# Block 0 of a fused linear-attention and hard-swish kernel: chunks 2 and 3 read in parts, the second pair's down product by seven products

## The chip, the cores and the metric

The kernel runs on one core of a Trainium2 chip. The metric is the device time of one execution in microseconds. Engines are named as in the profile: PE (TensorE, matmuls), PEld (its weight loads), DVE (VectorE), ACT (ScalarE), POOL (GpSimd), SP (SyncE, which issues nearly all DMAs). A line number such as L824 is a line of the kernel before the change.

## The reference

Two parts are computed one after the other. The first is a recurrence over 768 tokens for 4 batches and 8 heads of 48 elements; the second is a feed-forward layer over the 3072 resulting tokens with 384 inputs and 2048 hidden columns.

```
for t in range(S):
    cur = einsum('bhd,bhe->bhde', u * k[t], v[t])
    y[t] = einsum('bhd,bhde->bhe', r[t], state + cur)
    state = w[t][..., None] * state + einsum('bhd,bhe->bhde', k[t], v[t])
x = y as (3072, 384)
h = x @ w_in                      # 384 x 2048
g = h * clip(h + 3, 0, 6) / 6
out = g @ w_out                   # 2048 x 384
```

All data are in 32-bit floats, except that the two weight matrices arrive as 64-bit floats, which the kernel turns into 32-bit floats itself.

## The kernel before

**Tiling.** The 3072 tokens are 24 chunks of 128 (`L`); `NT` is 24, the chunk's index is `i`. Two batches run side by side, so chunks 0 and 1 are both the first of their batch (`is_first`). Four chunks make a block (`BC`), so there are six blocks (`bk`). A chunk's 8 heads lie as 4 pairs (`P`) on 112 partitions: head 2p on partitions 0 to 47 and head 2p+1 on partitions 64 to 111.

**A chunk.** Its steps have short names in the planner, with the index behind: `feat` and `tok` load it; `back` and `fore` are two scans on DVE (L422, L431) that give the running products of the decays; `K` and `R` multiply them in (L442, L446; on DVE for chunks 0 to 6, on POOL after that); `own`, `dot`, `sum` and `diag` make the diagonal (L455, L465, L471, L481); `score` multiplies keys with queries (L490) and `above` copies the upper triangle into the matrix A (L497); `turn` and `turned` transpose K; `kv` makes the chunk's own outer products (L590), `kvs` takes them out of PSUM (L601, or L599), and `decay`, `mid`, `decb` and `state` update the state (L519, L527, L535). The result y is the sum of a product with the state (`read_state`, L568) and one with the values (`read_values`, L577), and `leave` copies it to `xT`, the input of the feed-forward layer.

**Where y goes.** `xT` has three column tiles of 128 rows, and the last of the four head pairs has to be spread over them. A block has two ways for this. Chunks 0 and 1 of block 0 (those below `BY_SUM`) go by parts: `first` computes the last pair alone (`read_last`), `third` copies it out on ACT (`leave_last`), and `read` (`read_rest`) adds it to the other three pairs by six matmuls with a selection matrix (L649), followed by the state and value products of the three pairs. All other chunks are read in one run and left as four copies (L677), and when both chunks of a pair are there, six small DMAs on SP (`last_pair`, L684; steps `move`) bring the last pair's rows to their places.

**The kv product.** Where a chunk is in `SOLO`, its `kv` is a step of its own; otherwise it is done at the end of the `read` of an earlier chunk, in free columns of that chunk's PSUM tile `y_ps`. Chunk 1 (`KV_APART`) has its own in two PSUM banks and two copies out (L599).

**The feed-forward layer in blocks 1 to 5.** The up product goes by 20 products instead of 24 per half (`up_product`, L824), for which DVE makes sums of the weights once (`sum_w`, L770 to L776; steps `sin0` to `sin20`) and sums of the inputs per block (`sum_x`; steps `tx`). The sums whose target is a `w` place overwrite `w_in` and wait until block 0's up products are all done. The down product is taken for two chunks at a time (a pair `p`) by seven products of half width instead of eight (`down_product`, L879), with sums of the weights (`sum_out`, L800; steps `sout1` to `sout4`, two halves each) and sums of the activations per pair (`sum_g`, L864; four kinds, two halves each), and seven reads (`down_read`; one copy L888, four scaled copies L895, two on DVE L897). `sout3` overwrites a part of `w_out` and waits for all plain down products of block 0.

**The feed-forward layer in block 0.** It goes the plain way: `up` (L710) for 16 row groups f and two pairs of chunks, `ramp` (L700) and `gate` (L721), then `down` (L729): for each of the four chunks 16 matmuls of 384 columns, and `drain` (L736) and `store`. Every 32-bit matmul shows as two instructions in the profile.

**What sets the order.** `Plan.order` is a list scheduler: each step has an engine, an assumed duration, what it follows, a key (a due time) and the buffers that it holds; among the steps that could start first on an engine it takes the one with the smallest key. Keys come from constants at the top (`START` for chunks 0 to 5, `OWN` for the diagonal, `CONV` for the weights' conversion, `UP` for block 0's up products, `SUMS` for the weights' sums, `LAG`, `AHEAD`, `LEAD`, `READ`, `GATE`, `TX` for the later blocks). `Plan.emit` writes the steps out in that order, and until block 0's first up product it puts dummy matmuls (`spin`, L1247) where the plan shows PE idle: `FILL` times the hole, divided by `SPIN` (0.25 us).

```
for _ in range(int(self.FILL * (self.start[n] - last) / self.SPIN) if n != self.until else 0):
    self.spin()
```

The tile of the selection matrix and the tile of the activations' sums share the one buffer `S_`; the gated activations of a block lie in two large tiles `g0` and `g1`, which the next block's up product fills again.

Of the kernel before, what the change touches and what calls it, by code (L numbers as in the profile page):

```python
# [18 lines left out]
L = 128  # L19
# [5 lines left out]
GBC = 3  # L25


LAG = 12.679
AHEAD = -7.562
LEAD = 5.403  # L30
BEHIND = (-1, -1, -1, 0, 6, 7)
BY_PE = 9
OWN = -16.106
SOLO = (0, 1, 2, 3, 4, 5)
EARLY = 7
APART = 1
KV_APART = (1,)
BY_SUM = 2
START = (-165.91, -200.65, -51.72, -167.86, 44.69, 31.26)
CONV = (-77.31, 6.92)  # L40
UP = (-66.42, 3.35, 14.73, 4.86)
SUMS = (157.11, 42.24, -10.72)
READ = 4.918
GATE = 10.716
TX = -15.408
LEAST = 2.0 ** -60


# [186 lines left out]
def fast_path(tc, feat, tok, wflat, ub, ug, moe_w_in, moe_w_out, out, flag, n_chunks):  # L235
# [21 lines left out]
    with ExitStack() as ctx:  # L257
# [283 lines left out]
        def new_y(i, alone=False):  # L541
            started = set()
            if i == APART and not alone:
                st[i].update(started=started, y_ps=[bank()[:, :P * HL].rearrange("q (p t) -> q p t", p=P) for _ in range(2)])
                return
            y_ps = pp.tile([128, 2, 512], F32, name="y_ps")
            if not alone:
                y_ = y_ps[:, :, :P * HL].rearrange("q a (p t) -> q a p t", p=P)
                st[i].update(started=started, y_ps=[y_[:, a] for a in range(2)], y_all=y_)
            j = i if alone else i + 1 if i < BC else i + 2  # L550
            if j < NT and (alone or j not in SOLO):
# [28 lines left out]
        def write(i):  # L580
            d = st[i]
            for p in range(P):
                for a in range(1 if is_last(i) else 2):
                    for g in range(2):

                        half = slice(a * HL, (a + 1) * HL)
                        cols = slice(g * GP, GP if g == 0 else PR)
                        fresh = (a, g * GP) not in d["kv_started"]
                        d["kv_started"].add((a, g * GP))
                        nc.tensor.matmul(d["kv_ps"][a][cols, p, :] if i in KV_APART else d["kv_ps"][cols, a, p, :], lhsT=d["kn"][half, p, cols],  # L590
                                         rhs=d["v"][half, 2 * p + g, :], start=fresh, stop=True, skip_group_check=True)

        def written(i):
            d = st[i]
            m = 1 if is_last(i) else 2
            d["kvs"] = wk.tile([PR, 2, P, D], F32, name="kvs", bufs=1)
            if i in KV_APART:
                for a in range(m):
                    nc.scalar.copy(out=d["kvs"][:, a], in_=d["kv_ps"][a])  # L599
                return  # L600
            nc.scalar.copy(out=d["kvs"][:, :m].rearrange("q a p e -> q a (p e)"),  # L601
                           in_=d["kv_ps"][:, :m].rearrange("q a p e -> q a (p e)"))

        def write_alone(i):
            if i in KV_APART:
                st[i].update(kv_started=set(), kv_ps=[bank()[:PR, :P * D].rearrange("q (p e) -> q p e", p=P) for _ in range(2)])
            else:
                new_y(i, True)
            write(i)

        def begin(i):
# [57 lines left out]

        def leave(i):  # L670
            bk, c = divmod(i, BC)
# [179 lines left out]
        def sum_g(bk, p, k, x):  # L851

            b = blocks[bk]
            m = HF // 2
            if k == 1 and x == 0:
                b["S", p] = wk.tile([128, HF, L], F32, name="S_", bufs=1)
            S = b["S", p][:, x * m:(x + 1) * m, :]

            def part(h, c):
                return b["g", p][:, h * HF + x * m:h * HF + (x + 1) * m, c * L:(c + 1) * L]  # L860
            (a11, a21), (a12, a22) = ([part(h, c) for c in range(2)] for h in range(2))
            o, x0, x1, op = {1: (S, a21, a22, ALU.add), 2: (S, S, a11, ALU.subtract), 3: (a21, a11, a21, ALU.subtract),
                             4: (S, a12, S, ALU.subtract)}[k]
            nc.vector.tensor_tensor(out=o, in0=x0, in1=x1, op=op)  # L864
# [93 lines left out]
        def do(fn, *args):  # L958
            return lambda: fn(*args)
# [25 lines left out]
        for i in range(NT):  # L985
# [40 lines left out]
            plan.add(f"turned{i}", "ACT", 0.42, do(turned_k, i), [turned_by(i)] + [f"turned{i - 1}"] * (i > 0), due - 2 if i > BC + 1 else due + 0.5,  # L1026
                     [("kn", [written_by(i)])])
            if i in SOLO:
                plan.add(f"kv{i}", "PE", 0.5, do(write_alone, i), [f"turned{i}", f"tok{i}"], t - 0.2,
                         [("bank", [f"kvs{i}"])] * 2 if i in KV_APART else [("y", [f"kvs{i}"])])  # L1030
            plan.add(f"kvs{i}", "ACT", 0.37 if i not in KV_APART else 0.5, do(written, i), [written_by(i)], t - 6 if i >= len(START) else t - 0.5,
                     [("kvs", [f"decb{i}"] if last else [f"state{i}"])])
            S_ = [("S", [f"read{i}" if i < BC else f"begin{i}"] + [f"state{i}"] * (not last))]
            if not first:
# [12 lines left out]
            y = [("y", [f"leave{i}"] + [f"kvs{with_}"] * (with_ < NT and with_ not in SOLO))]  # L1047
            if i == APART:
                y = [("bank", [f"leave{i}"])] * 2
            if i < BY_SUM:  # L1050
                plan.add(f"first{i}", "PE", 0.65 if first else 0.75, do(read_last, i), [f"above{i}", f"decb{i}"], t + 0.01, y)
                plan.add(f"third{i}", "ACT", 0.54 if i != APART else 0.9, do(leave_last, i), [f"first{i}"], t + 0.01,
                         ([("x", all_up), ("S_", [f"read{j}" for j in range(BY_SUM)])] if i == 0 else []))
# [21 lines left out]
            if c % 2 and i >= BY_SUM:  # L1075
                for g in range(2):
                    plan.add(f"move{bk}.{c // 2}.{g}", "SP", 1.8, do(last_pair, bk, c - 1, c + 1, g, nc.sync),
                             [f"leave{i - 1}", f"leave{i}"], when(i) - 50, kb=1, dmas=3)

        plan.add("u", "SP", 0.45, load_u, ["fetch3"], -60.0, kb=320)  # L1080
        plan.add("later", "SP", 0.45, load_rest, ["feat0"], key=-999.0, kb=630)
# [10 lines left out]
                plan.add(f"full{j}", "DVE", 0.87, do(high_low, j), [f"join{j}", f"whole{j}"], t, port=True)  # L1092
        ready = "full" if f64 else "fetch"

        classic = range(BC)
        all_down = [f"down0.{c}.{q}" for c in classic for q in range(HF)]
        part_of = {c: c0 for c0, c1 in parts for c in range(c0, c1)}
        for x, (c0, c1) in enumerate(parts):
            m = c1 - c0
            for f in range(NFC):  # L1100
                k = UP[2 * x] + f * UP[2 * x + 1]
                n_ = f"0.{f}.{c0}"
                plan.add(f"up{n_}", "PE", 0.645 * m, do(up, f, c0, c1), [f"{ready}{f // 2}"] + [f"leave{j}" for j in range(c0, c1)] + [f"move0.1.{g}" for g in range(2)] * (c0 >= BY_SUM),
                         k, [("bank", [f"gate{n_}"])])
                plan.add(f"ramp{n_}", "ACT", 0.1 + 0.135 * m, do(ramp, f, c0, c1), [f"up{n_}"], k - 3, [("clip", [f"gate{n_}"])])
                plan.add(f"gate{n_}", "DVE", 0.07 + 0.134 * m, do(gate, f, c0, c1),
# [37 lines left out]
        for bk in range(NB):  # L1144
# [7 lines left out]
            for d in range(2 * (bk > 0)):  # L1152
# [39 lines left out]
                for x in range(8):  # L1192
# [394 lines left out]
```

## Time and profile before

| | |
|---|---|
| median of three runs | 559.42 us (557.51 to 560.03) |
| the profiled execution | 560.03 us; its span 558.3 us |
| busy: PE / DVE / ACT / POOL | 543.8 / 435.8 / 265.2 / 108.2 us |
| mean granted PE clock | 0.982 |
| first up product of block 1 | at 145.8 us |

The span is the time from the first to the last instruction; the rest, 1.7 us, lies around it. PE counts as busy while it works at half clock and while a pipelined matmul waits inside it, and the dummy matmuls count too. Nearly the whole of what the change touches lies before 148 us, in block 0.

### The profile page before, as it was taken

What the parts mean: (1) busy time and instruction counts of PE and PEld (TensorE: products, weight loads), DVE (VectorE), ACT (ScalarE), POOL (GpSimd) and SP (SyncE); (2) the same over time, 40 slices, a digit from 0 to 9 for tenths busy, and PEclk for the clock granted to TensorE, in tenths of its full rate; (3) what the DMA queues carried; (4) which work ended last, traced back from release to release, by engine and by line L of the source; (5) the groups of instructions that cost most, each with busy time, mean ns of one, the idle gap of its engine ahead of it and who ended that gap; (6) DMA issues with size and microseconds to landing.
All of it is one profiled execution on the core that took longest, in us unless ns stands there. A gap on an engine that the chain in (4) does not pass through costs nothing.

```text
span 558.3 us, 13179 instructions
## 1 busy us (share of the span) xinstructions
PE 543.8 (97%) x5460; PEld 477.0 (85%) x5460; DVE 435.8 (78%) x717; ACT 265.2 (48%) x653; POOL 108.2 (19%) x111
## 2 busy tenths in 40 slices
PE   8999999999999999999999999999899999999996
PEld 8888766777688899888999888999788899988995
DVE  7969999999989967889968899967967817087440
ACT  3868782456377415456516456525447520255100
POOL 2000000046165015202053026232401000000000
PEclk9869999999999999999999999999989999999998
DMA  8948941633243282466335694036300000100001
GB/s 275 297 131 212 296 167 43 177 107 112 81 120 100 95 227 75 134 225 166 92 83 185 221 266 123 20 116 206 91 1 7 4 8 15 43 1 1 1 15 48
DMA packets 23269, 64.06 MB, mean 115 GB/s; under 512 B 3216, under 2 KB 10544, under 8 KB 23200
## 3 DMA queue, kind: packets, MB, share of 16 engines
q1 hardware_dynamic: 23072, 63.12, 37.8%
q8 instruction: 45, 0.74, 0.6%
q14 instruction: 24, 0.20, 0.1%
q10 hardware_dynamic: 128, 0.00, 0.0%
HBM read 57.31 MB, written 4.72 MB: 111 GB/s over the span
## 4 chain that ended last, share of the span: by engine, by line
PE 81%; DVE 11%; DMA 3%; ACT 2%; issue 1%; POOL 0%; DVEq 0%; POOLq 0%; ACTq 0%
PE bank L824 26%; PE bank L879 26%; PE bankS L824 5%; PE bankS L879 5%; PE bank L710 4%; PE bank L729 3%; DMA bits<-in_moe_w_out_dram 3%; PE bank L490 2%; PE y_ps L568 2%; PE y_ps L590 2%; PE bankS L1247 2%; PE ps L506 2%; PE y_ps L577 2%; PE ps L465 1%; DVE E L422 1%
## 5 line engine op out<-in xcount | busy, mean ns | idle before, releaser
L845 ACT ACTIVATE clip<-g,three 128x512 f32<-128x512 f32 x80 | 56.6, 720 | 44.5 <-DVE g L841 30.9
L841 DVE TENSOR_TENSOR g<-bank,g 128x512 f32<-128x512 f32 x80 | 53.7, 683 | 14.4 <-PE bank L824 10.7
L849 DVE SCALAR_TENSOR_TENSOR g<-clip,g 128x512 f32<-128x512 f32 x80 | 55.9, 714 | 7.3 <-ACT clip L845 7.3
L879 PE MATMUL bank<-w_out,g 128*128 128x192 f32 x320 | 56.7, 327 | 0.0
L879 PEld LDWEIGHTS bank<-w_out,g 128*128 128x128 f32 x320 | 52.8, 190 | 0.6
L442 POOL TENSOR_TENSOR K<-feat_in,E 112x512 f32<-112x512 f32 x17 | 22.0, 1293 | 150.0 <-DVE rk L455 100.4
L481 ACT ACTIVATE A<-eyes,dg 128x64 f32<-128x64 f32 x192 | 48.9, 335 | 1.5 <-PE y_ps L577 0.9
L710 PE MATMUL bank<-xT,w_in 128*128 128x256 f32 x192 | 47.4, 397 | 0.8 <-DMA xT<-xT 0.8
L677 ACT COPY xT<-y_ps 48x256 f32<-48x256 f32 x88 | 32.2, 366 | 31.8 <-PE y_ps L577 30.8
L729 PE MATMUL bank<-w_out,g 128*128 128x384 f32 x128 | 45.0, 493 | 0.3 <-DVE w_out L409 0.3
L710 PEld LDWEIGHTS bank<-xT,w_in 128*128 128x128 f32 x192 | 36.9, 198 | 8.9 <-DVE g L721 1.6
L895 ACT ACTIVATE o<-bank 128x192 f32<-128x192 f32 x30 | 9.9, 330 | 69.9 <-PE bank L879 69.9
L824 PE MATMUL bank<-xT,w_in 128*128 128x256 f32 x160 | 41.1, 380 | 0.0
L446 POOL TENSOR_TENSOR W<-feat_in,W 112x512 f32<-112x512 f32 x17 | 24.1, 1419 | 86.3 <-DVE W L431 86.3
L839 ACT COPY g<-bank 128x512 f32<-128x512 f32 x50 | 29.0, 580 | 18.7 <-PE bank L824 18.6
L729 PEld LDWEIGHTS bank<-w_out,g 128*128 128x128 f32 x128 | 23.4, 190 | 13.5 <-DVE w_out L409 0.4
L824 PEld LDWEIGHTS bank<-xT,w_in 128*128 128x128 f32 x160 | 30.2, 190 | 4.1
L422 DVE TENSOR_TENSOR_SCAN E<-feat_in,back 112x520 f32<-112x520 f32 x24 | 30.9, 1288 | 2.9 <-POOL K L442 1.6
L824 PE MATMUL bank<-xT,bits 128*128 128x256 f32 x120 | 31.0, 381 | 0.0
L431 DVE TENSOR_TENSOR_SCAN W<-feat_in,start 112x520 f32<-112x520 f32 x24 | 30.4, 1268 | 0.8 <-PE y_ps L568 0.7
L879 PE MATMUL bankS<-w_out,g 128*128 128x192 f32 x160 | 28.0, 328 | 0.4 <-ACT bankS L888 0.4
L879 PE MATMUL bank<-more,g 128*128 128x192 f32 x160 | 28.1, 328 | 0.0
(279 smaller groups left out, 1140.7 us busy)
## 6 DMA issues: line engine op xcount, KB each, us to landing
feat_in<-in_feat_dram SPq DMA_DIRECT2D x23, 675.9 KB, 6.7
bits<-in_moe_w_in_dram SPq DMA_DIRECT2D x8, 768.0 KB, 7.5
bits<-in_moe_w_out_dram SPq DMA_DIRECT2D x8, 768.0 KB, 6.5
feat_in<-in_moe_w_in_dram SPq DMA_DIRECT2D x8, 768.0 KB, 4.4
feat_in<-in_moe_w_out_dram SPq DMA_DIRECT2D x8, 768.0 KB, 4.4
rk_in<-in_tok_dram SPq DMA_DIRECT2D x15, 384.0 KB, 6.0
v_in<-in_tok_dram SPq DMA_DIRECT2D x24, 192.0 KB, 4.2
out_dram<-o SPq DMA_DIRECT2D x24, 192.0 KB, 2.1
```

Source lines behind the costliest of these rows:

```text
L422: nc.vector.tensor_tensor_scan(out=E_[:, ::-1], data0=d["w"][:, :0:-1], data1=back.rearrange("q p t -> q (p t)")[:, ::-1], initial=0.0, op ...
L431: nc.vector.tensor_tensor_scan(out=W_, data0=d["w"][:, :-1], data1=starts[i % 2].rearrange("q p t -> q (p t)"), initial=0.0, op0=ALU.mult, ...
L481: nc.scalar.activation(out=d["A"][:, h, :], in_=eyes, func=ACT.Copy, scale=d["dg"][:, h])
L677: nc.scalar.copy(out=blocks[bk]["xT"][g * GP:g * GP + D, :, at:at + HL], in_=st[i]["y_ps"][a][(g ^ a) * GP:(g ^ a) * GP + D, :, :])
L710: nc.tensor.matmul(h_ps[:, :(c1 - c0) * L], lhsT=w_in[:, f // 2, j, f % 2, :], rhs=b["xT"][:, j, c0 * L:c1 * L], start=(j == 0), stop=(j = ...
L729: nc.tensor.matmul(b["o", c][:, :DM], lhsT=g_of(0, f, c), rhs=w_out[:, f, :], start=(f == 0), stop=(f == NFC - 1))
L824: nc.tensor.matmul(b["p", d, c][:, z * HB:(z + 1) * HB], lhsT=weight(W_PLACE[r])[:, 2 * z + d, :], rhs=x_at(bk, X_PLACE[r]), start=fresh a ...
L839: nc.scalar.copy(out=out_, in_=src)
L841: nc.vector.tensor_tensor(out=out_, in0=src, in1=out_of(bk, d, other), op=ALU.add if sign > 0 else ALU.subtract)
L845: nc.scalar.activation(out=c, in_=out_of(bk, d, u), func=ACT.Relu, bias=three, scale=1.0)
L849: nc.vector.scalar_tensor_tensor(out=g, in0=blocks[bk]["r", d, u], scalar=6.0, in1=g, op0=ALU.min, op1=ALU.mult)
L879: nc.tensor.matmul(b["d", p, to][:, :h], lhsT=a, rhs=w(), start=(f == 0 and k in (1, 5)), stop=(f == HF - 1 and k in (2, 3, 4)), skip_grou ...
```

## The change

The chunks 2 and 3 of block 0 are now read by parts, like 0 and 1 (`first`, `third`, `read_rest`, `leave_rest`), and block 0's six small DMAs are gone; `read_both` and `BY_SUM` go with them. The down product of block 0 stays plain for chunks 0 and 1 (`classic`); chunks 2 and 3 are computed by seven products, with the four activation sums and the seven reads of such a pair. `sout3` therefore waits for the plain down products of two chunks and stands before a product of block 0. Chunk 1 leaves `SOLO` and `KV_APART`: its `kv` is done at the end of chunk 0's `read`. Eleven of the constants for the keys change. `FILL` and `SPIN` are the same in both kernels.

```diff
-LAG = 12.679
-AHEAD = -7.562
-LEAD = 5.403
+LAG = 11.816
+AHEAD = -12.641
+LEAD = 3.239
-OWN = -16.106
-SOLO = (0, 1, 2, 3, 4, 5)
+OWN = -1.171
+SOLO = (0, 2, 3, 4, 5)
-KV_APART = (1,)
-BY_SUM = 2
-START = (-165.91, -200.65, -51.72, -167.86, 44.69, 31.26)
-CONV = (-77.31, 6.92)
-UP = (-66.42, 3.35, 14.73, 4.86)
-SUMS = (157.11, 42.24, -10.72)
-READ = 4.918
-GATE = 10.716
-TX = -15.408
+START = (-122.25, -133.43, -35.45, -193.52, 38.16, -10.0)
+CONV = (-81.21, 7.03)
+UP = (-62.25, 2.9, -5.61, 5.34)
+SUMS = (187.95, 20.98, 24.5)
+READ = 2.945
+GATE = 9.211
+TX = 13.253
...
         def write_alone(i):
-            if i in KV_APART:
-                st[i].update(kv_started=set(), kv_ps=[bank()[:PR, :P * D].rearrange("q (p e) -> q p e", p=P) for _ in range(2)])
-            else:
-                new_y(i, True)
+            new_y(i, True)
             write(i)
...
-        def read_both(i):
-            new_y(i)
-            read_state(i, range(P))
-            nc.tensor.drain()
-            read_values(i, range(P))
...
             def part(h, c):
+                if bk == 0:
+                    return b["g", h][:, x * m:(x + 1) * m, (2 * p + c) * L:(2 * p + c + 1) * L]
                 return b["g", p][:, h * HF + x * m:h * HF + (x + 1) * m, c * L:(c + 1) * L]
...
-            if i < BY_SUM:
+            if bk == 0:
                 plan.add(f"first{i}", "PE", 0.65 if first else 0.75, do(read_last, i), [f"above{i}", f"decb{i}"], t + 0.01, y)
...
-            elif bk == 0:
-                plan.add(f"read{i}", "PE", 1.5, do(read_both, i), [f"above{i}", f"decb{i}"], t + 0.01, y)
-                plan.add(f"leave{i}", "ACT", 1.5, do(leave, i), [f"read{i}"], t + 0.02)
...
-        classic = range(BC)
-        all_down = [f"down0.{c}.{q}" for c in classic for q in range(HF)]
+        classic = range(2)
+        all_down = [f"down0.{c}.{q}" for c in classic for q in range(HF)] + [f"down0.1.{k_}.{x}" for k_ in range(1, 8) for x in range(2)]
...
-            for p in range(2 * (bk > 0)):
-                at = K + U_ + D_ * p
+            for p in range(bk == 0, 2):
+                at = K + U_ + D_ * p if bk else D0 * 1.5
 
                 def gated(f0, f1):
+                    if bk == 0:
+                        return [f"gate0.{f}.{part_of[c]}" for f in range(f0, f1) for c in (2, 3)]
                     return [f"gate{bk}.{f % HF // 4}.{2 * (f % 4) + p}" for f in range(f0, f1)]
```

More of the change, by code (lines that the diff above doesn't have):

```diff
@@ L550, in new_y @@
             j = i if alone else i + 1 if i < BC else i + 2
-            if j < NT and (alone or j not in SOLO):
+            if j < NT:
                 st[j]["kv_started"] = started
@@ L589, in write @@
                         d["kv_started"].add((a, g * GP))
-                        nc.tensor.matmul(d["kv_ps"][a][cols, p, :] if i in KV_APART else d["kv_ps"][cols, a, p, :], lhsT=d["kn"][half, p, cols],
+                        nc.tensor.matmul(d["kv_ps"][cols, a, p, :], lhsT=d["kn"][half, p, cols],
                                          rhs=d["v"][half, 2 * p + g, :], start=fresh, stop=True, skip_group_check=True)
@@ L596, in written @@
             d["kvs"] = wk.tile([PR, 2, P, D], F32, name="kvs", bufs=1)
-            if i in KV_APART:
-                for a in range(m):
-                    nc.scalar.copy(out=d["kvs"][:, a], in_=d["kv_ps"][a])
-                return
             nc.scalar.copy(out=d["kvs"][:, :m].rearrange("q a p e -> q a (p e)"),
@@ L604, in write_alone @@
         def write_alone(i):
-            if i in KV_APART:
-                st[i].update(kv_started=set(), kv_ps=[bank()[:PR, :P * D].rearrange("q (p e) -> q p e", p=P) for _ in range(2)])
-            else:
-                new_y(i, True)
+            new_y(i, True)
             write(i)
@@ L1028, in fast_path @@
             if i in SOLO:
-                plan.add(f"kv{i}", "PE", 0.5, do(write_alone, i), [f"turned{i}", f"tok{i}"], t - 0.2,
-                         [("bank", [f"kvs{i}"])] * 2 if i in KV_APART else [("y", [f"kvs{i}"])])
-            plan.add(f"kvs{i}", "ACT", 0.37 if i not in KV_APART else 0.5, do(written, i), [written_by(i)], t - 6 if i >= len(START) else t - 0.5,
+                plan.add(f"kv{i}", "PE", 0.5, do(write_alone, i), [f"turned{i}", f"tok{i}"], t - 0.2, [("y", [f"kvs{i}"])])
+            plan.add(f"kvs{i}", "ACT", 0.37, do(written, i), [written_by(i)], t - 6 if i >= len(START) else t - 0.5,
                      [("kvs", [f"decb{i}"] if last else [f"state{i}"])])
@@ L1049, in fast_path @@
                 y = [("bank", [f"leave{i}"])] * 2
-            if i < BY_SUM:
+            if bk == 0:
                 plan.add(f"first{i}", "PE", 0.65 if first else 0.75, do(read_last, i), [f"above{i}", f"decb{i}"], t + 0.01, y)
                 plan.add(f"third{i}", "ACT", 0.54 if i != APART else 0.9, do(leave_last, i), [f"first{i}"], t + 0.01,
-                         ([("x", all_up), ("S_", [f"read{j}" for j in range(BY_SUM)])] if i == 0 else []))
+                         ([("x", all_up), ("S_", [f"read{j}" for j in range(BC)])] if i == 0 else []))
                 plan.add(f"read{i}", "PE", (2.6 if first else 2.95) + 0.4 * (i + 1 not in SOLO), do(read_rest, i), [f"third{i}"] + [f"turned{i + 1}", f"tok{i + 1}"] * (i + 1 not in SOLO), t + 0.01)
                 plan.add(f"leave{i}", "ACT", 1.05, do(leave_rest, i), [f"read{i}"], t + 0.02)
-            elif bk == 0:
-                plan.add(f"read{i}", "PE", 1.5, do(read_both, i), [f"above{i}", f"decb{i}"], t + 0.01, y)
-                plan.add(f"leave{i}", "ACT", 1.5, do(leave, i), [f"read{i}"], t + 0.02)
             else:
@@ L1074, in fast_path @@
                 plan.add(f"leave{i}", "ACT", 1.5, do(leave, i), [f"read{i}"], t + 0.5, space)
[L1075 to L1078, printed above, removed]
+                if c % 2:
+                    for g in range(2):
+                        plan.add(f"move{bk}.{c // 2}.{g}", "SP", 1.8, do(last_pair, bk, c - 1, c + 1, g, nc.sync),
+                                 [f"leave{i - 1}", f"leave{i}"], when(i) - 50, kb=1, dmas=3)
         plan.add("u", "SP", 0.45, load_u, ["fetch3"], -60.0, kb=320)
@@ L1102, in fast_path @@
                 n_ = f"0.{f}.{c0}"
-                plan.add(f"up{n_}", "PE", 0.645 * m, do(up, f, c0, c1), [f"{ready}{f // 2}"] + [f"leave{j}" for j in range(c0, c1)] + [f"move0.1.{g}" for g in range(2)] * (c0 >= BY_SUM),
+                plan.add(f"up{n_}", "PE", 0.645 * m, do(up, f, c0, c1), [f"{ready}{f // 2}"] + [f"leave{j}" for j in range(c0, c1)],
                          k, [("bank", [f"gate{n_}"])])
```

## The prediction

> **What bounds the kernel now.** I read the page's busy times and slices first, then the busy time by stretch, then the chain of waits, and last the engines' instructions in order of time up to 150 us, since the change lies there.
>
> ```profile
> PE 543.8 (97%) x5460; PEld 477.0 (85%) x5460; DVE 435.8 (78%) x717; ACT 265.2 (48%) x653; POOL 108.2 (19%) x111
> ...
> PEclk9869999999999999999999999999989999999998
> ```
>
> From this alone PE bounds everything. By stretch (length, then busy PE, PEld, DVE, ACT, POOL) it looks different:
>
> ```profile
> 22.00:37.00 15.00, 14.12 (x83) 12.69 (x84) 12.46 (x18) 8.47 (x33) 0.00 (x0) 0.54 0.51 174
> 40.00:100.00 60.00, 57.69 (x570) 43.01 (x569) 56.71 (x99) 39.46 (x85) 0.00 (x0) 1.00 0.63 189
> 100.00:148.00 48.00, 47.69 (x668) 33.76 (x666) 45.33 (x79) 22.88 (x73) 16.30 (x14) 1.00 0.45 124
> 148.00:232.00 84.00, 83.36 (x906) 75.73 (x909) 69.56 (x106) 41.10 (x105) 29.69 (x28) 1.00 0.40 118
> ```
>
> Up to 148 us DVE is as full as PE: it idles 3.3 us in 40 to 100 and 2.7 us in 100 to 148. In block 1 (148 to 232) it idles 14.4 us. From 22 to 37 PE runs at a mean clock of 0.54. The chain of waits (start, length) says who ends block 0:
>
> ```profile
> 126.31 3.90 PE bank L710 x18
> 130.24 0.48 ACT clip L700
> 130.74 0.42 DVE g L721
> ...
> 136.05 1.12 DVE w_in L774
> 137.19 0.70 DVE w_in L776
> 137.92 0.69 DVE w_in L774
> ...
> 146.65 0.43 DVE T__1761 L774
> ```
>
> After the last up product at 130 us, DVE alone carries the chain: nine in-place weight sums, then the eleven input sums of block 1. PE meanwhile has down products in stock and waits for nothing:
>
> ```profile
> 134.08 11.88 PE L729 MATMUL bank<-w_out,g 128*128 128x384 f32 x36
> 145.80 1.03 PE L824 MATMUL bank<-T__1761,bits 128*128 128x256 f32 x4
> ```
>
> So in block 0 a microsecond on DVE counts, one on PE counts less, and in blocks 1 to 5 PE counts.
>
> **PE, part by part.** Removed: the plain down of two chunks, 64 instructions. The run above gives 11.88 / 36 = 0.33 us each, 21.1 us. Added: seven products of 16 instructions, 112 in all; eight of them take 1.30 us in the chain (L879), 18.2 us. Gain 2.9 us. Added too: the selection matmuls of chunks 2 and 3. Chunk 0's twelve stand from 18.88 to 20.26, 1.38 us, so 2.8 us. The state and value products are the same in number, only split. Two more drains and the splitting cost between 0 and 0.4 us per chunk (0.4 is the gap that chunk 0's parts show around a drain); other PE work can stand there, I take 0. PE's balance is -0.1 us: nothing.
>
> **DVE.** Added: eight activation sums of 128x512. The same L864 in block 1 takes 0.69 us: 5.5 us. Two reads of L897 at 0.357: 0.7 us. The last two weight sums of w_out (`sout3`) run today at 149.6 and 151.6, after block 0; they become a condition of block 0's seventh product, so 2 x 0.92 = 1.8 us move into the full stretch. Nothing goes. Together 8.0 us.
>
> What can leave the stretch? The keys of later chunks' scans become about 6 us later (AHEAD 5.1, LAG 0.9). Chunk 9's forward scan (131.54, 1.23 us) and chunk 10's backward scan with its reciprocal (132.94, 2.23 + 0.21 us) are used first by chunk 8's read and begin, at 152.7 and 148.7 us, long before block 2 needs that chunk (232 us). That is 3.7 us that block 1, with DVE idle for 14.4 us, could take. Bounds: 0 to 3.7; I take all, since nothing that ends block 0 hangs on them, and chunk 8's begin can shift with them. DVE's own idle time of 2.7 us in 100 to 148 can be filled partly: bounds 0 to 2.7, I take 1.0, since these are single holes of 0.3 to 0.8 us behind other engines.
>
> **ACT.** Two drains of 0.49 us go; one copy of 0.30 and four of 0.33 come: +0.6 us. Third and leave of a chunk (0.53 + 0.32 + 0.64) equal the four copies before (1.50). ACT idles 25 of the 48 us up to 148: nothing. Should that cover go, it costs 0.6.
>
> **SP.** The six small DMAs go. Their issue held the queue for 1.96 us at 55.03 and 3.35 us at 57.89, and the weight fetch at 62.71 stood behind the second lot. Waits seen in that region: PE 0.79 us on those DMAs at 65.08, DVE 0.84 us on the fetched weights at 59.65. Bounds -1.6 to 0; I take 0, since DVE has other conversions and gates there (9.55 of 10 us busy from 60 to 70) and the fetches are next limited by three buffers.
>
> **Chunk 1's kv.** Today it stands apart at 15.75 to 16.35 and its copy (0.52) and decay (0.36) are done by 19.1, before `first1` starts at 21.27. Now it follows chunk 0's read, which ended at about 21.5: 0.6 us for the product, 0.47 for the copy, 0.36 for the decay, with hops some 23.4 us. `first1` comes up to 2.1 us later. Behind it stand `third1`, the rest of chunk 1's read and then the first up product (32.16). But `third1` today waits on ACT until 23.12 anyway, and chunk 2's dots and spins fill PE to 25.9. Bounds 0 to +2.1; I take +1.0.
>
> **The clock.** It falls to half from 22.9 to 36.6 us, 13.7 us, worth 6.85 us of PE time.
>
> ```profile
> 21.00:22.00 1.00, 0.89 (x36) 0.59 (x36) 0.86 (x2) 0.97 (x2) 0.00 (x0) 1.00 0.98 238
> 22.00:23.00 1.00, 0.23 (x1) 0.23 (x2) 1.00 (x3) 0.95 (x4) 0.00 (x0) 0.87 1.05 246
> 23.00:24.00 1.00, 1.00 (x6) 1.00 (x6) 0.97 (x2) 0.74 (x5) 0.00 (x0) 0.50 1.05 331
> ```
>
> The row: one hole of 0.8 us after a stretch of small matmuls was followed by half clock. The Trainium skill, in "TensorE: Matmul & The Clock Gate", Part 1, states that the clock falls after an idle window of about 3.4 us; by this rule neither kernel should lose anything here, and the sum would fall by the whole throttled part. The measurement contradicts it, so this is left out of the sum. In the changed kernel the place is still thin (a wait for chunk 1's kv), though the planner puts spins into holes that it foresees. I take the same loss as before, 0; the ends are a full gain and one stretch of half clock longer by a quarter (+1.7).
>
> **Sum.** 8.0 - 3.7 - 1.0 + 1.0 - 0.1, about +4.2 us (with nothing for SP, ACT and clock). On the profiled execution (span 558.3 and 1.7 around it, 560.0) that is 564.2; this execution is the slowest of three, 0.6 above the median of 559.4, so the forecast is 563.6.
>
> **The rivals.** *Faster: the clock stays up.* Chunk 1 waits longer in the plan, so more spins stand between 16 and 25 us, and the half clock of 13.7 us never comes. For it: spins kept full clock until 22.8. Against it: the hole at 22 came from an `own` on DVE that was late, which a plan does not foresee. PE would win 6.85, but DVE only its idle time of 22 to 40 us, 2.5 + 1.6 = 4.2. The point that decides is whether PE sees a hole like that of 22 us. With SP's 1.6: 563.6 - 1.0 - 4.2 - 1.6 = 556.8; with the rest of DVE's holes (1.7) filled too, 555.1.
>
> *No difference.* The sums go into all of DVE's holes (2.7), chunk 1's delay costs nothing, SP gives 0.8: 8.0 - 3.7 - 2.7 - 0.8 = +0.8, so 560.2. Here also belongs that the change doesn't do what its description says: it speaks of holes filled wholly, but both constants for this are equal in the two kernels, so the 82 spin instructions change only by the plan's holes.
>
> *Much slower: block 1 waits for the `g` tiles.* Block 1's first copies into them (148.33 today) must follow the last of seven products, and those stand behind sums (kinds 2 and 4) that wait for earlier products and for DVE. PE then stands once its banks are full. It decides when the last two products (2.6 us each) come behind the input sums: 563.6 + 5.2 = 568.8. For it: DVE is full there. Against it: today PE had 11.9 us of down products ready at this place, and a planner sees these dependencies.
>
> **How the numbers follow.** A measurement of this kernel tells 0.5%, 2.8 us, from no change. Chances: forecast 0.45 (562.2 to 567), block 1 waits 0.13, no difference 0.23, clock 0.19. So slower 0.58, same 0.23, faster 0.19. The upper end is all of DVE's 8.0, 2.1 for chunk 1 and 1.7 for the clock: 571.2. The lower is 555.1. The range is 555.5 to 571. The forecast's own range, with its case alone, is 562.2 to 567.
>
> **What would show it.** Right: DVE busy above 45.3 us of 48 before block 1's first up product, this product at 149 to 151 us instead of 145.8, chunk 9's and 10's scans after it; L864 40 to 48 times and L729 64 times; spans from there to the end equal to today's 412 us within 2 us. Wrong: a granted clock of 1.0 throughout 20 to 40 us, first up product (32.16) 3 us or more earlier, or a long PE idle ahead of block 1's reads. What would make the prediction wrong above all is the keys: they rearrange all blocks, and PE idles or waits for some 8 us in blocks 1 to 5, which I hold constant.

## The result, and the profile after

The changed kernel takes 565.67 us (median of five runs, 565.11 to 566.47), the kernel before 557.76 (five runs, 556.99 to 560.03). The ratio is 1.0132, with a 95% interval of 1.0105 to 1.0159: 1.3% slower, some 7.4 us. The forecast was 563.6, its range 555.5 to 571. The forecast had counted on 4.2 us more than the kernel before. That its number is only 2.1 us off is partly luck: it started from 559.42 us, the median of three runs, and the five runs here have a median 1.7 us lower.

The profiled execution of the changed kernel took 566.47 us, its span is 564.6 us. Line numbers of the changed kernel are some 2 to 15 lower: L809 is the up product of blocks 1 to 5, L866 the down product by seven, L851 the activation sums, L785 the sums of `w_out`, L884 the two reads on DVE. Where the time went is seen when the span is cut at the start of block 1's first up product. Busy time by stretch of the kernel before (stretch, length, then PE, PEld, DVE, ACT, POOL, clock, DMA share, GB/s), cut there at 145.80 us:

```profile
0.00:145.80 145.80, 140.84 (x1627) 109.30 (x1628) 132.13 (x222) 85.56 (x224) 20.33 (x29) 0.95 0.61 180
145.80:558.30 412.50, 402.95 (x3835) 367.74 (x3833) 303.63 (x496) 179.67 (x429) 87.84 (x82) 0.99 0.30 92
```

and of the changed kernel, cut at 152.25 us, with the stretch up to 148 us as in the prediction:

```profile
0.00:152.25 152.25, 145.64 (x1749) 120.89 (x1749) 141.29 (x235) 87.77 (x230) 21.56 (x29) 0.96 0.57 172
152.25:564.60 412.35, 400.92 (x3800) 365.70 (x3798) 306.09 (x494) 178.12 (x427) 88.96 (x82) 1.00 0.30 92
...
100.00:148.00 48.00, 45.66 (x669) 37.32 (x668) 47.55 (x71) 20.80 (x64) 18.55 (x14) 1.00 0.37 102
```

The rest of the span is as long as before, 412.35 us against 412.50; the stretch ahead of that product is 6.45 us longer. There DVE has 9.16 us more to do and idles 10.96 us instead of 13.67 (9.16 - 2.71 = 6.45); from 100 to 148 it idles 0.45 us. Such a sum comes out for every engine, since its busy and its idle time make up the stretch: PE has 4.80 us more to do there and idles 1.65 us more. It doesn't tell which of them makes the stretch longer.

The equal length of the second stretch hides two things. PE has 2.03 us less to do in it, because chunk 8's first products now stand ahead of the cut, and it idles 1.88 us more. At the starts of blocks 2, 3 and 4 it waits 1.1, 1.0 and 1.7 us for DVE's input sums, where the kernel before has waits of 0.2, 0.2 and 0.5 us.

The chain of waits of the changed kernel at the end of block 0 (start, length) shows DVE in nearly every piece. PE comes in with the last product, which waits for a read on DVE (L884), and ends the chain:

```profile
138.08 1.28 DVE S__1409 L851
139.37 1.42 DVE w_in L761
...
140.81 1.37 DVE w_in L759
142.18 1.58 DVE w_in L757
...
147.14 0.68 DVE w_in L757
147.82 0.55 DVE o L884 x2
148.37 0.04 issue
148.41 2.87 PE bank L866 x16
```

PE's instructions show the same place from the other side (in brackets the idle time ahead of an instruction, and what ended it):

```profile
130.29 1.56 PE L695 MATMUL bank<-xT,w_in 128*128 128x256 f32 x6 [1.03 <-DVE g L706]
...
145.08 1.57 PE L866 MATMUL bank<-w_out,S__1409 128*128 128x192 f32 x8 [1.26 <-DVE S__1409 L851]
146.48 1.46 PE L866 MATMUL bank<-w_out,g 128*128 128x192 f32 x8
148.41 2.87 PE L866 MATMUL bank<-more,g 128*128 128x192 f32 x16 [0.47 <-DVE o L884]
...
152.25 1.04 PE L809 MATMUL bank<-T__1819,bits 128*128 128x256 f32 x4
```

PE waits for DVE three times, 2.76 us in all, and from 148.41 on it works without a wait up to the first up product. That product needs from DVE the first four of block 1's eleven input sums (`X_PARTS` in the kernel), and they are ready at 151.14 us, 1.1 us ahead of it. In the kernel before they are ready at 144.35 us, with the end of this instruction:

```profile
143.93 0.42 DVE L772 SCALAR_TENSOR_TENSOR T__1761<-xT,T__1761 128x256 f32<-128x256 f32 x1
```

That is 1.4 us ahead of the up product at 145.80, and PE has no wait from 100 us up to it. So in the kernel before PE's own run of work ends block 0, and DVE is done 1.4 us earlier. In the changed kernel DVE keeps PE waiting up to 148.4, and PE's last product follows.

The DVE instructions in order of time show why the added work is 9.2 us and not 8.0. The same sum of 128x512 takes 0.68 us in one place and 1.4 to 1.6 in another:

```profile
110.26 1.46 DVE L851 TENSOR_TENSOR S__1409<-g,g 128x512 f32<-128x512 f32 x1
111.75 1.56 DVE L851 TENSOR_TENSOR g<-g 128x512 f32<-128x512 f32 x1
...
122.33 2.79 DVE L785 TENSOR_TENSOR w_out<-w_out 128x768 f32<-128x768 f32 x2
...
134.34 0.68 DVE L851 TENSOR_TENSOR S__1409<-g,S__1409 128x512 f32<-128x512 f32 x1
```

and POOL's instructions lie just beside the long ones:

```profile
109.99 1.18 POOL L444 TENSOR_TENSOR W<-feat_in,W 112x512 f32<-112x512 f32 x1 [1.18 <-DVE W L429]
111.22 1.54 POOL L440 TENSOR_TENSOR K<-feat_in,E 112x512 f32<-112x512 f32 x1
122.50 1.81 POOL L444 TENSOR_TENSOR W<-feat_in,W 112x512 f32<-112x512 f32 x1 [9.74 <-DVE W L429]
124.27 1.22 POOL L517 TENSOR_TENSOR S<-S,w_min 112x192 f32<-112x192 f32 x1
```

Up to the cut, the eight sums take 7.8 us, `sout3` 2.8 and the two reads 0.6 on DVE. Of the other groups one has a piece more, the state update (L533, nine instead of eight); the rest are the same in number, among them 11 backward and 10 forward scans in both kernels.

### The profile page after: what moved, and what is told of

Same layout as the page of the kernel before. It is cut to its first block, busy times and chain, and to the rows that moved or that the text cites. A ratio compares the mean times of both kernels' runs of the same rounds, so it can differ in the third digit from the quotient of the medians.

```text
span 564.6 us, 13346 instructions
## 1 busy us (share of the span) xinstructions
PE 546.6 (97%) x5546; PEld 486.6 (86%) x5546; DVE 447.4 (79%) x727; ACT 265.9 (47%) x657; POOL 110.5 (20%) x111
## 4 chain that ended last, share of the span: by engine, by line
PE 66%; DVE 25%; DMA 2%; issue 2%; ACT 2%; SPq 0%; POOL 0%; DVEq 0%; POOLq 0%
PE bank L866 23%; PE bank L809 21%; PE bankS L866 5%; PE bank L695 4%; PE bankS L809 4%; DMA xT<-xT 2%; DVE g L826 2%; PE bankS L1232 2%; DVE W L429 2%; DVE E L420 2%; DVE top L402 2%; PE bank L488 2%; DVE g L834 1%; PE y_ps L566 1%; PE ps L504 1%
## 5 line engine op out<-in xcount | busy, mean ns | idle before, releaser
L866 PE MATMUL bank<-w_out,g 128*128 128x192 f32 x352 | 63.3, 327 | 0.0
L834 DVE SCALAR_TENSOR_TENSOR g<-clip,g 128x512 f32<-128x512 f32 x80 | 57.7, 732 | 6.0 <-ACT clip L830 6.0
L866 PEld LDWEIGHTS bank<-w_out,g 128*128 128x128 f32 x352 | 58.0, 190 | 0.7
L662 ACT COPY xT<-y_ps 48x256 f32<-48x256 f32 x80 | 29.2, 365 | 28.7 <-PE y_ps L575 27.9
L809 PE MATMUL bank<-xT,w_in 128*128 128x256 f32 x160 | 41.5, 382 | 0.6 <-DVE g L826 0.6
L444 POOL TENSOR_TENSOR W<-feat_in,W 112x512 f32<-112x512 f32 x17 | 22.0, 1293 | 68.1 <-DVE W L429 68.1
L809 PEld LDWEIGHTS bank<-xT,w_in 128*128 128x128 f32 x160 | 29.8, 190 | 5.3 <-DVE g L826 1.4
L809 PE MATMUL bank<-xT,bits 128*128 128x256 f32 x120 | 31.1, 381 | 0.0
L866 PE MATMUL bank<-more,g 128*128 128x192 f32 x176 | 30.5, 327 | 0.5 <-DVE o L884 0.5
L866 PE MATMUL bankS<-w_out,g 128*128 128x192 f32 x176 | 30.9, 327 | 0.0
L866 PEld LDWEIGHTS bank<-more,g 128*128 128x128 f32 x176 | 28.6, 190 | 0.8 <-DVE o L884 0.8
L866 PEld LDWEIGHTS bankS<-w_out,g 128*128 128x128 f32 x176 | 28.7, 190 | 0.1
```

What stands on the lines that cost most here:

```text
L444: early(i).tensor_mul(d["R"], d["r"], d["R"])
L662: nc.scalar.copy(out=blocks[bk]["xT"][g * GP:g * GP + D, :, at:at + HL], in_=st[i]["y_ps"][a][(g ^ a) * GP:(g ^ a) * GP + D, :, :])
L809: nc.tensor.matmul(b["p", d, c][:, z * HB:(z + 1) * HB], lhsT=weight(W_PLACE[r])[:, 2 * z + d, :], rhs=x_at(bk, X_PLACE[r]), start=fresh a ...
L834: nc.vector.scalar_tensor_tensor(out=g, in0=blocks[bk]["r", d, u], scalar=6.0, in1=g, op0=ALU.min, op1=ALU.mult)
L866: nc.tensor.matmul(b["d", p, to][:, :h], lhsT=a, rhs=w(), start=(f == 0 and k in (1, 5)), stop=(f == HF - 1 and k in (2, 3, 4)), skip_grou ...
```

## The experiments

Each ratio is to the kernel before, measured alongside on the same chip at 556.7 to 558.3 us (median); kernels that were measured at different times are compared by their ratios.

**1. DVE's sums taken away, order kept.** In `sum_g` and `down_product`:

```
...
-            nc.vector.tensor_tensor(out=o, in0=x0, in1=x1, op=op)
+            if bk:
+                nc.vector.tensor_tensor(out=o, in0=x0, in1=x1, op=op)
...
-                S = b["S", p][:, f, :] if ("S", p) in b else None
+                S = (b["S", p][:, f, :] if bk else a11) if ("S", p) in b else None
```

> The changed kernel in its own order, but the eight activation sums of block 0 are not issued; the products read a gated activation in their place, so block 0's second pair gives other numbers. PE's work is the same. DVE theory: DVE has 7.8 us less in front of block 1's first up product, but holes come back: 558.5 to 561. If PE's dependencies among the seven products set the end, the time falls by 1.3 us (the longest wait of PE for a sum) to 2: 563.5 to 564.5.

561.83 us, ratio 1.0055 (1.0027 to 1.0082), against the changed kernel's 1.0132 (1.0105 to 1.0159): the sums cost about 0.8%, 4.3 us of the 7.4; from the two intervals this is uncertain by some 2.2 us either way. In the profiles half of it lies ahead of the cut: the first up product of block 1 comes at 150.04 instead of 152.25. The other half lies behind it: the rest of the span is 409.96 instead of 412.35, and the waits for DVE at the starts of blocks 2 to 4 are 0.2, 0.7 and 0.6 us instead of 1.1, 1.0 and 1.7. DVE has 6.4 us less to do ahead of the cut, of which 4.2 come back as holes. PE waits only 0.45 us for DVE from 100 us to the up product, instead of 2.76, and is the last there (145.42 of 150.04 us busy). So in the changed kernel DVE's work holds block 0 up by 2 us, and below that stands PE's own limit, at 150 us.

**2. PE's work taken away, order kept.** In `down_product`:

```
-            for f in range(x * m, (x + 1) * m):
+            for f in range(x * m, (x + 1) * m if bk or k not in (6, 7) else x * m):
```

> The changed kernel in its own order, but two of block 0's seven products (the sixth and the seventh, four halves of 1.3 us) issue no matmul, so chunks 2 and 3 give other numbers. PE has 5.2 us less to do, DVE the same. If DVE ends block 0, nearly nothing is won: block 1's first up product at 151 to 152.3 us, the time 0 to 1.5 us below the changed kernel (564 to 566). If PE's balance is the bound, 561 or less.

565.08 us, ratio 1.0158 (1.0117 to 1.0199): nothing won. PE's instructions in order of time show where the 5.2 us went:

```profile
137.96 1.57 PE L866 MATMUL bank<-w_out,S__1409 128*128 128x192 f32 x8
144.69 2.93 PE L866 MATMUL bank<-w_out,S__1409 128*128 128x192 f32 x8 [5.16 <-DVE S__1409 L851]
148.40 5.21 PE L866 MATMUL bank<-more,g 128*128 128x192 f32 x16 [0.79 <-DVE o L884]
```

PE now waits 5.16 us for the last activation sum, where the changed kernel waits 1.26 us, and the sum is ready at the same time (144.6 against 145.0 us). The last product starts at 148.40, at the same instant as in the changed kernel: DVE's sum and read set it, although PE had 5.2 us less to do ahead of them. The comparison has a flaw that I had not foreseen: the hole brought the clock down (0.50 from 145 to 150 us), so the products after it took 2.93 us instead of 1.57 and 5.21 instead of 2.87. With that the first up product came at 154.57, 2.3 us later than in the changed kernel, against my expectation, and the rest of the span was 3.8 us shorter. At full clock the last product could have started some 0.3 us earlier at most, by an estimate from DVE's rows: the weights' sum ahead of its read ends at 147.43, and the read started at 147.72.

**3. Both taken away.** The two edits together.

> Both left out at once: the eight activation sums and the two products, order kept. Leaving out the sums alone gave a first up product at 150.0 us with PE full behind it (47.6 of 48 us). If DVE and PE are two limits close behind each other, both together win clearly more than the sums alone: first up product at 145 to 147.5 us and 557.5 to 560. If something else holds block 0 at 150, as the sums alone: 561 to 562.

562.85 us, ratio 1.0126 (1.0084 to 1.0168). The first up product comes at 148.5 us in the profile, later than I expected, and the time shows no gain over the sums alone. The granted clock of these four runs was 0.974 to 0.983, lower than in experiment 1 (0.982 to 0.990), and again it fell in a hole (0.82 and 0.84 from 140 to 150 us). PE waits 3.38 us for DVE's read, and the last product then takes 4.55 us instead of 2.87. At full clock the first up product would have come at some 146.8 us, an estimate from these two durations, and within what I expected. The times alone decide nothing on the two limits.

**4. DVE's work added to the kernel before, order kept.** Behind eight of the weights' sums:

```
+            if n in (0, 2, 4, 6, 8, 10, 12, 14):
...
+                nc.vector.tensor_tensor(out=w_tiles["extra"][:, n // 2 % 2 * 4:n // 2 % 2 * 4 + 4, :], in0=weight("w10"), in1=weight("w11"), op=ALU.add)
```

> The kernel before in its own order, with eight more sums of 128x512 on DVE between the weights' sums, whose results nobody reads: only DVE time, 5.5 us at 0.69 us each, up to 7.8 at what the changed kernel showed. DVE theory: +4 to +6.5, so 562 to 564.5. If DVE is not what ends block 0, below +1: 558 to 559.

562.44 us, ratio 1.0034 (0.9994 to 1.0075): +1.9 us, between -0.3 and +4.2. This number mixes runs at different clocks. Among the 28 runs of the two kernels here, those with 0.01 more mean clock are some 4.5 us faster; compared at equal clock, the added work costs 3.6 us (2.7 to 4.5). The two profiled executions, both at a clock of 0.982, took 565.47 and 560.03 us. The eight sums took 5.5 us as reckoned, and the profile has the first up product at 149.05 instead of 145.80, 3.25 us later, now behind a wait for DVE:

```profile
149.05 1.10 PE L828 MATMUL bank<-T__1770,bits 128*128 128x256 f32 x4 [1.59 <-DVE T__1770 L772]
```

The fourth input sum ends at 148.90 instead of 144.35 us, 4.5 later. Of this, 1.3 us cost nothing: the time by which DVE was done ahead of the product in the kernel before. So there DVE's time counts, but only after that lead is used up: a miss for my picture of that kernel, in which every microsecond on DVE counted.

**5. The shift that the prediction counted on.** `["tx1.3"]` added to what chunk 9's `fore` and chunk 10's `back` follow:

> The kernel before, with chunk 9's forward and chunk 10's backward scan made to follow the last input sum of block 1: the shift of 3.7 us that the prediction counted on, alone. If the scans can leave the full stretch at no cost, the first up product comes 2 to 3.5 us earlier and the time is 555 to 557. If block 1 needs them, the gain is given back in block 1: 558 to 560 with the first up product earlier all the same.

557.30 us, ratio 1.0007 (0.9984 to 1.0031); the first up product at 146.2 us. Its DVE instructions show both scans behind the input sums, as meant, yet the last input sum ends at 146.5 us, only 0.6 us earlier than in the kernel before (147.1). Other steps moved up into the room (a reduction, L473, and two sums, L527 and L535), and POOL's work now lies beside two of the weights' sums:

```profile
133.02 1.77 DVE L776 TENSOR_TENSOR w_in<-w_in 128x512 f32<-128x512 f32 x1
134.82 1.37 DVE L774 TENSOR_TENSOR w_in<-bits,apart 128x512 f32<-128x512 f32 x1
```

Besides, PE could not have used an earlier end: the four sums that the first up product needs are ready at 143.7 us (144.35 before), while PE's run of 36 down products ends at 146.4 us and touches the product. So moving these scans is worth nothing here, since PE ends this stretch.

**6. The clock in the kernel before.** In `Plan.emit`:

```
+            for _ in range({"dot2": 4}.get(n, 0)):
+                self.spin()
             emit()
```

> The kernel before with four dummy matmuls more, ahead of chunk 2's dot, where the trace shows PE's hole of 0.8 us at 22.0 us and half clock from 22.9 to 36.6. The four fill some 0.9 us. If the hole is what brings the clock down, the mean granted clock rises from 0.982 to 0.99 or more, the first up product of block 1 comes 2 to 5 us earlier and the time is 2 to 5 us below before, 552 to 555: better than both kernels. If the clock falls for the small matmuls around it, or if DVE ends block 0 anyhow, nothing changes: within 1.5 us of before.

553.64 us, ratio 0.9939 (0.9919 to 0.9959): 3.4 us faster than the kernel before, and better than both. The granted clock is 0.994 to 0.999 in ten of its eleven runs, where the kernel before had 0.985 to 0.993 alongside; at the slope of the last section, 4.6 us for each 0.01 of clock, this is worth some 4 us, about what was won. The eleventh run is the profiled one: there the clock fell at 15 us already and stayed down for 27 us, and it took 565.9 us.

```profile
15.00:42.00 27.00, 26.62 (x241) 23.64 (x242) 19.79 (x31) 14.15 (x43) 0.00 (x0) 0.50 0.57 160
```

**7. The clock in the changed kernel.** The same edit with `{"first1": 3, "dot2": 2, "dot4": 2}`:

> The changed kernel with dummy matmuls more in the three holes ahead of its two half-clock stretches (27.8 to 37.5 and 72 to 75.8 us): three ahead of chunk 1's first read, two ahead of chunk 2's dot, two ahead of chunk 4's dot. If DVE ends block 0 by 2 us, a kept clock wins at most what the early up products bring DVE, 0 to 2 us: 563.5 to 566. If the clock were the loss, 560 or less.

566.38 us, ratio 1.0178 (1.0145 to 1.0210): nothing won, though the clock was 0.991 to 0.994 in all four runs, against 0.982 to 0.990 in the changed kernel's five, and the second stretch of half clock was gone. Half a per cent of clock is some 3 us of PE time; it is not in the time. The profile shows that something was won and lost again. The first up product of block 0 comes 1.3 us earlier (31.7 against 33.0), and at 50 us DVE is 2.0 us ahead of the changed kernel, by the same instruction. Then PE stands still, and the profile names nothing that it waits for:

```profile
54.69 0.20 PE L590 MATMUL y_ps<-v_in,kn 64*48 64x48 f32 x1 [2.45 <-issue]
```

The clock halves behind this hole for some 3 us, DVE idles 3.65 of the 10 us from 50 to 60, and from 100 us on it is 1.6 us late; the first up product of block 1 comes at 153.80 instead of 152.25. What the hole comes from stays open, and whether the other three runs had it isn't known. So this run doesn't tell whether a kept clock is worth something in the changed kernel.

**8. Both edits of 5 and 6.**

> The kernel before with both: the four dummy matmuls ahead of chunk 2's dot, which brought 0.6%, and the two scans after block 1's input sums, which brought nothing alone. If PE ends block 0 in the kernel before and DVE stands close behind, the kept clock makes DVE the last, and now the shift of its 3.7 us pays: 1 to 3 us below the 553.6 of the dummies alone, 550.5 to 552.5. If the scans are needed where they stand, or block 1 gives the gain back: 553 to 555.

553.73 us, ratio 0.9946 (0.9919 to 0.9973): the same as the dummies alone. In its profile (553.91 us) the clock falls for a few microseconds only, the first up product of block 0 comes at 28.0 us and that of block 1 at 141.54, each 4.2 us earlier than in the kernel before, and the latter again follows PE's plain down products without a gap:

```profile
22.00:37.00 15.00, 14.54 (x113) 12.83 (x112) 14.36 (x22) 12.44 (x39) 0.00 (x0) 0.89 0.81 254
...
129.82 11.88 PE L731 MATMUL bank<-w_out,g 128*128 128x384 f32 x36
141.54 1.03 PE L826 MATMUL bank<-T__1764,bits 128*128 128x256 f32 x4
```

DVE's input sums end at 141.8 us there, 5.3 us earlier than in the kernel before: the earlier up products brought DVE's whole chain forward too. The four sums that the up product needs are ready at 139.06, 2.5 us ahead of it, so PE ends block 0 with the clock kept, too.

**9. One part of the change at a time.** Here the planner made a new order each time.

Chunks 2 and 3 by parts alone, in the kernel before (`BY_SUM = 4`):

> The kernel before with chunks 2 and 3 read by parts, without the six small DMAs, alone; its own keys. PE gets 2.6 us more (the selection matmuls as the changed kernel's trace shows them), DVE nothing. If PE and DVE end block 0 together in the kernel before (PE's last plain down product ends at 146.0 us), the first up product comes 2 to 5 us later, at 148 to 151, and the time is 560 to 563; a second half-clock stretch near 70 us would come along. If only DVE counted: 556 to 558.5.

565.32 us, ratio 1.0151 (1.0118 to 1.0183): as much as the whole change, and more than I expected. The profile (the fastest of its five runs, 561.18) has the first up product at 150.4 us, behind PE's last plain down product at 149.5. The half clock near 70 us did not come along in this run, which has the highest clock of the five (0.989; the others, 0.980 to 0.984, took 564.5 to 567.8 us).

The new keys alone, in the kernel before:

> The kernel before with the eleven new keys alone, its structure as it was. If the keys carry the loss, 564 to 566 as the changed kernel. If the structure's DVE work carries it, 556 to 560. The two runs that mixed one kernel's structure with the other's keys (577.7 and 584.3) speak for a third case: keys fit one structure, and the mixture is worse than both, 570 or more.

574.67 us, ratio 1.0317 (1.0281 to 1.0352): the third case. The first up product comes at 149.4 us, and block 1 takes 89.3 and block 2 93.2 us, where the kernel before has 85.0 and 83.2 from one block's first product with input sums to the next one's.

Seven products alone, in the kernel before:

> The kernel before with one part of the change alone: seven products for chunks 2 and 3. DVE theory: DVE has some 9 us more to do ahead of block 1's first up product, of which its holes take 2 to 3, so +5.5 to +7: 563.5 to 565. Theory of the keys: 558 or less, because PE has 2.9 us less to do.

584.32 us, ratio 1.0444 (1.0387 to 1.0501). The first up product comes at 165.4 us; from 148 to 170 us PE is busy for 14.7 of 22 us, at a clock of 0.77.

The changed kernel with the plain down product for all four chunks:

> The changed kernel with the plain down product for all four chunks of block 0; parts reading, joined kv and new keys stay. If DVE's added work (11.1 us of durations: sums 7.8, sout3 2.7, reads 0.6) is what moved block 1's first up product from 145.8 to 152.3 us, it goes back to about 146 to 147 and the time to 558.5 to 560.5. If the new keys or chunk 1's kv did it, the time stays at 564 to 566. If PE's balance decided, it gets 2.9 us slower: 568.

577.71 us, ratio 1.0354 (1.0303 to 1.0406), slower than the changed kernel, where I expected 6 us less. Block 0 does get shorter, to 150.2 us, but blocks 1 and 2 take 89.0 and 93.5 us, as with the new keys alone.

So the parts don't add up: alone they cost 1.5, 3.2 and 4.4%, together 1.3%. With keys chosen for another structure the planner's order was worse than both kernels in three of the four runs, and about as slow as the changed kernel in the fourth. Such a run doesn't price a part. Chunk 1's kv alone was not tried.

## Why the prediction was right, and where it was wrong

**What ends block 0.** The prediction said that in block 0 a microsecond on DVE counts and one on PE counts less. For the changed kernel that holds: the sums away, -4.3 us; products away, PE runs into a wait for DVE, and the time stays. For the kernel before it is wrong in its order: there PE ends block 0, and DVE is done 1.4 us earlier. PE's clock kept won 3.4 us; DVE loaded by 5.5 us delayed the product by 3.25, since the lead went first. The change turned this round: DVE's four sums are ready 6.8 us later, and the product comes 6.45 us later. The forecast put DVE's time at its full price from the start, and its sum still came out near, because the lead is small. I had read the chain of waits, where DVE stands in the last pieces, and had taken the run of 36 down products, which ends at 146.0 us and touches the first up product, for work in stock that fills PE's time; PE had to do it before block 1 in any case.

**DVE's added work: mis-sized.** Predicted 8.0 us; the groups show 11.2 us of durations (sums 7.8 instead of 5.5, `sout3` 2.8 instead of 1.8, reads 0.6 instead of 0.7), and busy time rose by 9.16, since neighbouring instructions overlap and others got shorter. The duration came from a row of block 1; in block 0 three of the eight sums and both halves of `sout3` meet POOL and take about twice as long. The median of a row is no price where a second engine works beside it.

**The shift of 3.7 us: failed.** Chunk 9's and 10's scans stand at 135.2 and 136.4 us in the changed kernel, still ahead of the cut, although their keys are later. A key says what goes first among steps that are ready, not that a step is held back.

**DVE's holes.** 1.0 us taken; of the 2.7 us of holes in 100 to 148, 2.2 were filled (0.45 are left). Up to the cut it is 2.71, so some of it lies ahead of 100 us. The three misses (0 for 3.7, 2.7 for 1.0, and 9.2 for 8.0) gave 6.45 us against 4.2. The sum came out near the truth partly because these errors stand against each other.

**PE's balance of -0.1: wrong.** Busy time rose by 4.8 us ahead of the cut, and by 2.8 us in the whole span. The seven products brought little: the plain ones of four chunks took 45.0 us, two plain ones and the seven 24.1 + 20.7 = 44.8, with half clock in one run of them. The selection matmuls took 6.7 instead of 4.1 us; the dummies took 15.4 instead of 13.9 us, and chunk 8's first products, which now come ahead of the cut, add to it. With DVE the last, less of PE's work alone won nothing (experiment 2), but the added work puts PE's own limit at 150 us (experiment 1) instead of 146.

**Chunk 1's kv: right in the end, not in the middle.** Its first read starts at 24.99 us instead of 21.27, later than the bound of 2.1; the first up product at 33.02 instead of 32.16, +0.9 against +1.0.

**The clock: right in sum.** Half clock now lies from 27.8 to 37.5 and from 72 to 75.8 us, 13.5 us in all against 13.7. The rival of a kept clock failed in its condition (the clock fell). In the kernel before a kept clock is worth 3.4 us; for the changed kernel experiment 7 leaves it open, since its profile lost the gain again at 52 us.

**The signs.** Those that came true: DVE busy for 47.55 of 48 us, L729 (in the changed kernel under another number) 64 times, and the rest of the span within 0.2 us. Those that didn't: the first up product came at 152.25, behind the 149 to 151 us that were named; chunk 9's and 10's scans stayed ahead of it; and the activation sums went from 80 to 88 instructions, not from 40 to 48, a miscount of the kernel before.

**The other rivals.** Block 1 did not wait for the `g` tiles: from its first up product to block 2's it takes 84.0 us, 1.0 less than before. Spin instructions went from 82 to 96, by the plan's holes alone, as the text said of the unchanged constants.

**What stays open** is how the 7.4 us divide among the parts. Shown is 4.3 us, within some 2.2, for the activation sums in the changed kernel's own order, half of it in blocks 2 to 4. The rest goes with PE's limit, which lies 4 us later, and no run takes that apart. What the parts reading and the joined kv cost with keys chosen for them, no run here tells.

## What to carry to other kernels

Where two engines are nearly level, look at both ends: the chain of waits names one, but an uninterrupted run of work on the other that touches the same instant is a limit too. Find the instruction that both must wait for, ask what exactly it needs, and note when each engine has its part ready: the difference is a lead that work can use up for nothing. To price a part in a kernel whose order comes from a planner, leave its instructions out and keep the order; a run with a new order mostly measures the order. Compare runs at equal clock: an added 5.5 us looked like 1.9 here and was 3.6. And before trading work between engines, look at the clock: four dummy matmuls in one hole won 3.4 us here, where the change lost 7.4.

## What the hardware showed

The granted clock halved after holes of less than a microsecond among small matmuls (0.8 us at 22.0 in the kernel before; 0.71 and 0.35 us at 24.3 and 25.7 in the changed one), and filling one such hole kept it up in ten of eleven runs. The Trainium skill, "TensorE: Matmul & The Clock Gate", Part 1, gives an idle window of about 3.4 us as the condition; these runs show the fall without any idle time of that length. A longer hole did it too: behind the 5.16 us of experiment 2 the clock was 0.50 from 145 to 150 us. Over 62 runs of the kernel before, the time falls by 4.6 us for each 0.01 of mean clock (correlation -0.85), so its spread between runs goes with the clock. That the length of the one stretch at half clock makes this spread isn't shown; only one of these runs has a trace.

Up to block 1's first up product, DVE's sums of two 128x512 operands took 0.64 to 0.69 us where no POOL work lay beside them. Beside POOL work most took 1.2 to 1.7 us, in both kernels. It isn't always DVE that waits: two such sums in the kernel before kept 0.68 us (at 128.03 and 128.63), and there POOL's own instruction (L459) took 2.20 us, where the median of its 15 times is 1.00.
